# Moving PE transposes in and out of a saturated matmul stream at both ends of a six-layer cross network, and issuing the last stores from three engines

## The chip, the cores and the metric

One core of a Trainium2 chip. The metric is the device time of one execution in microseconds (us), read as the median over several executions.

In the profile, PE is TensorE's matmuls, PEld its weight loads, DVE VectorE, ACT ScalarE, POOL GpSimd, SP SyncE. The letter q behind an engine means its sequencer. The "span" is the time from the first to the last instruction; the measured time of a profiled run is about 1.8 us longer than its span.

## The reference

```python
B, D, L = 16384, 1024, 6            # all tensors bfloat16
def reference(x0, ws, bs):          # x0 (B, D), ws (L, D, D), bs (L, D)
    x = x0
    for l in range(ws.shape[0]):
        x = x0 * (x @ ws[l] + bs[l]) + x
    return x
```

## The kernel before

The batch is cut into 16 blocks of 1024 rows. Everything is computed transposed: features lie on the partitions and batch rows in the free dimension, so that the output of one layer is directly the moving operand of the next. A block has two halves of 512 rows (`bc`) and eight output groups (`nt`) per half. A group is eight accumulating matmuls of 128x512 into one PSUM bank, followed by two DVE operations.

```python
def layer(blk, l, x0T, src, dst, o_nat):
    for bc in range(BC):                       # 2 halves of 512 rows
        cs = slice(bc * MM_N, (bc + 1) * MM_N)
        for nt in range(NT):                   # 8 output groups
            ps = psum.tile([P, MM_N], FP32, name="ps", tag="ps")   # 8 buffers, shared
            for kc in range(KT):               # 8 matmuls
                nc.tensor.matmul(ps[:], lhsT=w_sb[l][:, kc, nt * P : (nt + 1) * P],
                                 rhs=src[:, kc, cs], start=(kc == 0), stop=(kc == KT - 1))
            # DVE: tmp = (ps + bias) * x0T ;  dst = tmp + src
            ...
            if last_layer and last_blk:        # progressive transposes back to rows
                for m in range(MS):            # 4 row tiles of this half
                    if nt % TPB == 0:
                        pts[m] = psum.tile([P, TPB, P], BF16, name="pt", tag="ps")
                    nc.tensor.transpose(pts[m][:, nt % TPB, :], dst[:, nt, col : col + P], ident[:])
                    if nt % TPB == TPB - 1 or nt == NT - 1:
                        ...                    # stage tile "on" at the first
                        evac_copy(on[:, j0 : j0 + nj, :], pts[m][:, :nj, :])   # ACT, DVE in turn
                        if nt == NT - 1:
                            nc.sync.dma_start(out=out[r : r + P, :], in_=...)  # 256 KB
```

The other 15 blocks are transposed in and out by DMA, off the critical path. Only the first block's input is transposed by TensorE, all of it ahead of the first layer:

```python
for s in range(MS): load_rows(s)               # row tiles 0..3, 256 KB each, on SP
load_w(0, 0, half)                             # first half of W0, 1 MB
load_w(0, half, D)                             # second half
for s in range(MS, BS): load_rows(s)           # row tiles 4..7
for l in range(1, L): load_w(l, 0, D)
...                                            # bias
for s in range(BS):
    pe_transpose_in(x0T_next, s, x0_rows[s])   # 8 transposes + one copy, per row tile
for blk in range(NBLK): ...                    # the layers
```

The scheduler of the compiler moves instructions within an engine. In the last layer it puts the four transposes of a group behind the sixth matmul of the next group, not directly behind their own.

## Time and profile before

| | before |
|---|---|
| median of 12 runs | 2689.27 us (2687.78 to 2689.86) |
| span of the profiled run | 2688.0 us |
| TensorE busy | 99% |
| first layer matmul | 17.74 us |
| full TensorE clock granted from | 20.09 us |
| last group's matmuls done to the end of the span | 7.5 us |

The time of the full clock is where the trace's clock record opens. It has no entry for the stretch before, and the page's PEclk row shows that stretch as full; that the clock was half there is read from the matmuls, which come every 0.43 us until then. (The prediction below says that the record "is 0.5"; it means this.)

From the page of the kernel before: the span, the busy shares, and the chain of work that ended last by engine and by line.

```profile
span 2688.0 us, 28374 instructions
...
PE 2654.2 (99%) x12177; PEld 1211.8 (45%) x12424; DVE 1811.0 (67%) x3081; ACT 9.2 (0%) x9; POOL 0.7 (0%) x6
...
PE 99%; issue 1%; DMA 0%; DVE 0%; ACTq 0%; ACT 0%
```

The matmul stream is the limit. In it one matmul follows another every 10.79/50 = 0.2158 us, and 12,288 of them make 2652 us. A change that keeps the matmuls can only act on the remaining 36 us at the two ends. The head is read from the chain of waits, kernel before, first 30 us (columns: start, duration, what):

```profile
3.52 1.06 PE pt L108 x9
4.59 9.72 DMA xn<-in_x_dram
14.31 0.05 issue
14.36 3.60 PE pt L108 x32
17.95 0.43 PE ps L133
```

TensorE waits for row tile 4 of x0 (`xn`) until 14.36, transposes rows 4 to 7 (L108, 32 transposes in 3.60 us on the slow clock), and only then starts layer 0 (L133). The landing events of the trace say that the first half of W0 had been there since 10.63 us.

The tail: the waits of TensorE in the kernel before, the whole span (columns: engine and line, what it waited for, us in total, times, longest; two lines of the start, 2.6 and 0.2 us, are left out).

```profile
PE pt L108 <- DMA xn<-in_x_dram: 7.6, 3, 6.2
PE pt L161 <- DVE xT L149: 4.4, 3, 1.8
```

The second line is three stalls of the last layer's transposes (L161): 1.30 us at 2645.3, 1.83 us at 2663.7 and 1.30 us at 2680.5. One regular step of the last layer, from the timeline of the kernel before (start, duration, engine, line, operation, in brackets the idle time before it and what ended it):

```profile
2668.95 0.23 PEld L161 LDWEIGHTS <-xT 128*128 128x128 bf16 x4 [0.50 <-DVE xT L149]
2668.96 0.40 PE L161 MATMUL pt<-ident,xT 128*128 128x128 bf16 x4
...
2669.19 1.89 PE L133 MATMUL ps<-xT,w 128*128 128x512 bf16 x8
...
2670.61 0.42 DVE L149 TENSOR_TENSOR xT<-tmp,xT 128x512 bf16<-128x512 bf16 x1
2671.09 0.23 PEld L161 LDWEIGHTS <-xT 128*128 128x128 bf16 x4 [0.50 <-DVE xT L149]
2671.09 0.40 PE L161 MATMUL pt<-ident,xT 128*128 128x128 bf16 x4
```

A step is 2671.09 - 2668.96 = 2.13 us for eight matmuls (8 x 0.2158 = 1.73 us) and four transposes. A matmul's bar is 0.38 us long though the next one can start 0.216 us later (its end is modelled).

### The profile page before, as it was taken

What the parts mean: (1) busy time and instruction counts of PE and PEld (TensorE: products, weight loads), DVE (VectorE), ACT (ScalarE), POOL (GpSimd) and SP (SyncE); (2) the same over time, 40 slices, a digit from 0 to 9 for tenths busy, and PEclk for the clock granted to TensorE, in tenths of its full rate; (3) what the DMA queues carried; (4) which work ended last, traced back from release to release, by engine and by line L of the source; (5) the groups of instructions that cost most, each with busy time, mean ns of one, the idle gap of its engine ahead of it and who ended that gap; (6) DMA issues with size and microseconds to landing.
All of it is one profiled execution on the core that took longest, in us unless ns stands there. A gap on an engine that the chain in (4) does not pass through costs nothing.

```text
span 2688.0 us, 28374 instructions
## 1 busy us (share of the span) xinstructions
PE 2654.2 (99%) x12177; PEld 1211.8 (45%) x12424; DVE 1811.0 (67%) x3081; ACT 9.2 (0%) x9; POOL 0.7 (0%) x6
## 2 busy tenths in 40 slices
PE   8999999999999999999999999999999999999998
PEld 4444444444444444444444444444444444444443
DVE  5666666666666666666666666666666666666665
ACT  0000000000000000000000000000000000000000
POOL 0000000000000000000000000000000000000000
PEclk9999999999999999999999999999999999999999
DMA  8030030300303012030120302203021030210200
GB/s 250 1 81 14 11 84 1 94 1 16 79 0 94 1 33 62 1 95 1 41 54 1 94 1 46 49 1 95 0 58 38 1 94 0 63 32 7 57 1 32
DMA packets 279962, 113.03 MB, mean 42 GB/s; under 512 B 255254, under 2 KB 257302, under 8 KB 279836
## 3 DMA queue, kind: packets, MB, share of 16 engines
q10 hardware_dynamic: 146412, 62.96, 9.5%
q1 hardware_dynamic: 133424, 48.24, 7.2%
q8 instruction: 97, 1.59, 0.3%
q14 instruction: 29, 0.24, 0.0%
HBM read 14.69 MB, written 33.55 MB: 18 GB/s over the span
## 4 chain that ended last, share of the span: by engine, by line
PE 99%; issue 1%; DMA 0%; DVE 0%; ACTq 0%; ACT 0%
PE ps L133 98%; DMA xn<-in_x_dram 0%; PE pt L161 0%; PE pt L108 0%; DVE tmp L141 0%; ACTq L229 0%; DVE on L100 0%; DVE xT L149 0%; ACT on L98 0%
## 5 line engine op out<-in xcount | busy, mean ns | idle before, releaser
L133 PE MATMUL ps<-xT,w 128*128 128x512 bf16 x10033 | 2204.0, 379 | 10.8
L133 PEld LDWEIGHTS <-w 128*128 128x128 bf16 x12288 | 1202.0, 98 | 1446.9 <-issue 1.5
L141 DVE SCALAR_TENSOR_TENSOR tmp<-ps,bias_sb,x0T 128x512 bf16<-128x512 f32 x1536 | 1153.2, 751 | 803.1 <-PE ps L133 771.6
L149 DVE TENSOR_TENSOR xT<-tmp,xT 128x512 bf16<-128x512 bf16 x1280 | 543.6, 425 | 44.0
L133 PE MATMUL ps<-x0T,w 128*128 128x512 bf16 x2008 | 443.5, 380 | 2.3 <-issue 0.2
L149 DVE TENSOR_TENSOR xT<-tmp,x0T 128x512 bf16<-128x512 bf16 x256 | 108.7, 425 | 8.8
L108 PE MATMUL pt<-ident,xn 128*128 128x128 bf16 x64 | 7.4, 313 | 7.6 <-DMA xn<-in_x_dram 7.6
L98 ACT COPY on<-pt 128x1024 bf16<-128x1024 bf16 x4 | 3.9, 1015 | 2661.9 <-PE pt L161 2661.9
L100 DVE COPY x0T<-pt 128x1024 bf16<-128x1024 bf16 x4 | 2.8, 692 | 12.7 <-PE pt L108 12.7
L161 PE MATMUL pt<-ident,xT 128*128 128x128 bf16 x64 | 6.4, 222 | 4.6 <-DVE xT L149 4.4
L108 PEld LDWEIGHTS <-xn 128*128 128x128 bf16 x64 | 6.6, 148 | 8.2 <-DMA xn<-in_x_dram 8.2
L161 PEld LDWEIGHTS <-xT 128*128 128x128 bf16 x64 | 3.6, 97 | 12.4 <-DVE xT L149 12.4
L98 ACT COPY x0T<-pt 128x1024 bf16<-128x1024 bf16 x4 | 4.1, 1013 | 11.5 <-PE pt L108 11.5
L100 DVE COPY on<-pt 128x1024 bf16<-128x1024 bf16 x4 | 2.7, 685 | 0.8 <-PE pt L161 0.8
L84 PE MATMUL bias_ps<-ident,bs_nat 6*128 6x6 bf16 x8 | 0.4, 165 | 2.6 <-DMA bs_nat<-in_bs_dram 2.6
L92 DVE COPY bias_sb<-bias_ps 128x48 f32<-128x48 f32 x1 | 0.2, 208 | 3.0 <-PE bias_ps L84 3.0
L84 PEld LDWEIGHTS <-bs_nat 6*128 6x128 bf16 x8 | 0.3, 101 | 2.6 <-DMA bs_nat<-in_bs_dram 2.6
L98 ACT ACT_TABLE_LOAD x1 | 1.3, 1283 | 1.4 <-PEq L218 1.4
masks.py:199 POOL TENSOR_SCALAR_AFFINE_SELECT ident<-ident 128x128 bf16<-128x128 bf16 x1 | 0.3, 295 | 0.1
masks.py:197 POOL MEMSET ident<- 128x128 bf16 x1 | 0.2, 205 | 0.3 <-POOLq L218 0.3
L218 POOL MEMSET const-bfloat16-1.0<- 128x1 bf16 x1 | 0.1, 103 | 0.0
L218 POOL MEMSET const-uint8-127<- 128x1 uint8 x1 | 0.1, 103 | 0.0
(2 smaller groups left out, 0.2 us busy)
## 6 DMA issues: line engine op xcount, KB each, us to landing
out_dram<-o_nat ACTq DMA_DIRECT2D x30, 1024.0 KB, 4.5
w<-in_ws_dram SPq DMA_DIRECT2D x5, 2048.0 KB, 19.9
o_nat<-xT ACTq DMA_TRANSPOSE x240, 2.4
xn<-in_x_dram SPq DMA_DIRECT2D x8, 256.0 KB, 4.6
w<-in_ws_dram SPq DMA_DIRECT2D x2, 1024.0 KB, 9.0
out_dram<-on SPq DMA_DIRECT2D x8, 256.0 KB, 2.3
x0T<-in_x_dram SPq DMA_TRANSPOSE x30, 7.9
bs_nat<-in_bs_dram ACTq DMA_DIRECT2D x1, 12.0 KB
```

What stands on the lines that cost most here:

```text
L84: nc.tensor.matmul(bias_ps[:, j, :], lhsT=bs_nat[:, j * P : (j + 1) * P], rhs=ident[0:L, 0:L], start=True, stop=True,)
L92: nc.vector.tensor_copy(out=bias_sb[:], in_=bias_ps[:])
L98: nc.scalar.copy(out=out_ap, in_=in_ap)
L100: nc.vector.tensor_copy(out=out_ap, in_=in_ap)
L108: nc.tensor.transpose(pt[:, jj, :], xn[:, (j0 + jj) * P : (j0 + jj + 1) * P], ident[:])
L133: nc.tensor.matmul(ps[:], lhsT=w_sb[l][:, kc, nt * P : (nt + 1) * P], rhs=src[:, kc, cs], start=(kc == 0), stop=(kc == KT - 1),)
L141: nc.vector.scalar_tensor_tensor(out=tmp[:], in0=ps[:], scalar=bias_sb[:, nt, l : l + 1], in1=x0T[:, nt, cs], op0=ALU.add, op1=ALU.mult,)
L149: nc.vector.tensor_tensor(out=dst[:, nt, cs], in0=tmp[:], in1=src[:, nt, cs], op=ALU.add)
L161: nc.tensor.transpose(pts[m][:, nt % TPB, :], dst[:, nt, col : col + P], ident[:])
L218: nc = _bacc.Bacc("TRN2", target_bir_lowering=False, num_devices=1)
```

## The change

Its intent is to start layer 0 as soon as rows 0 to 3 and W0 are there, and to transpose rows 4 to 7 inside layer 0's first half; to transpose the last layer's first half in one block; and to spread the last stores over three issuing engines. Eight stage buffers instead of four were meant to let rows 4 to 7 be requested early.

```diff
-    stage = ctx.enter_context(tc.tile_pool(name="stage", bufs=4))
+    stage = ctx.enter_context(tc.tile_pool(name="stage", bufs=8))
 ...
+    out_q = [nc.sync, nc.scalar, nc.gpsimd]        # store_rows(r, on): in turn
 ...   in layer():
+            progressive = last_layer and last_blk and bc == BC - 1
 ...
+                if after_group is not None and (bc, nt) in after_group:
+                    after_group[(bc, nt)]()
-                if last_layer and last_blk:
+                if progressive:                    # second half only
                     for m in range(MS):
 ...
-                            evac_copy(on[:, j0 : j0 + nj, :], pts[m][:, :nj, :])
+                            if nt == NT - 1 and m % 2 == 1:
+                                nc.vector.tensor_copy(out=on[...], in_=pts[m][...])
+                            else:
+                                nc.scalar.copy(out=on[...], in_=pts[m][...])
+                                store_rows(b0 + col, on)          # at nt == NT - 1
+            if last_layer and last_blk and not progressive:       # first half: one block
+                for m in range(MS):
+                    ...   # 8 transposes, one ACT copy, store_rows
 ...
-    for s in range(BS):
+    for s in range(MS):
         pe_transpose_in(x0T_next, s, x0_rows[s])
+    # rows 4..7: hooks of layer 0, first half, behind groups nt = 2, 3, 5, 6
+    after0 = {(0, nt): transposes of one row tile ...}
```

In the compiled order of the changed kernel, the block of 32 transposes has the 21 that do not need the half's last DVE result in front, and the other 11 behind them.

More of the change, by code (lines that the diff above doesn't have):

```diff
@@ L121, in load_block_T_dma, with store_rows, layer @@
         return x0T
-    def layer(blk, l, x0T, src, dst, o_nat):
+    out_q = [nc.sync, nc.scalar, nc.gpsimd]
+    out_rr = [0]
+    def store_rows(r, on):
+        q = out_q[out_rr[0] % len(out_q)]
+        out_rr[0] += 1
+        q.dma_start(out=out[r : r + P, :], in_=on[:].rearrange("p j c -> p (j c)"))
+    def layer(blk, l, x0T, src, dst, o_nat, after_group=None):
         last_layer = l == L - 1
@@ L167, in layer @@
                             if j0 == 0:
-                                on = stage.tile([P, KT, P], BF16, name="on", tag="xn")
-                                pts[(m, "on")] = on
+                                pts[(m, "on")] = stage.tile([P, KT, P], BF16, name="on", tag="xn")
                             on = pts[(m, "on")]
-                            evac_copy(on[:, j0 : j0 + nj, :], pts[m][:, :nj, :])
+                            if nt == NT - 1 and m % 2 == 1:
+                                nc.vector.tensor_copy(out=on[:, j0 : j0 + nj, :], in_=pts[m][:, :nj, :])
+                            else:
+                                nc.scalar.copy(out=on[:, j0 : j0 + nj, :], in_=pts[m][:, :nj, :])
                             if nt == NT - 1:
-                                r = b0 + col
-                                nc.sync.dma_start(
-                                    out=out[r : r + P, :],
-                                    in_=on[:].rearrange("p j c -> p (j c)"),
-                                )
+                                store_rows(b0 + col, on)
             if last_layer and not last_blk:
@@ L186, in layer @@
                 )
+            if last_layer and last_blk and not progressive:
+                for m in range(MS):
+                    col = bc * MM_N + m * P
+                    on = stage.tile([P, KT, P], BF16, name="on", tag="xn")
+                    for j0 in range(0, KT, TPB):
+                        nj = min(TPB, KT - j0)
+                        pt = psum.tile([P, TPB, P], BF16, name="pt", tag="ps")
+                        for jj in range(nj):
+                            nc.tensor.transpose(
+                                pt[:, jj, :], dst[:, j0 + jj, col : col + P], ident[:]
+                            )
+                        nc.scalar.copy(out=on[:, j0 : j0 + nj, :], in_=pt[:, :nj, :])
+                    store_rows(b0 + col, on)
     x0T_next = x0pool.tile([P, KT, Bb], BF16, name="x0T", tag="x0T")
-    for s in range(BS):
+    for s in range(MS):
         pe_transpose_in(x0T_next, s, x0_rows[s])
+    hooks0 = {}
+    rest = list(range(MS, BS))
+    if rest:
+        slots = [(0, nt) for nt in range(min(2, NT - 1), NT)]
+        for i, s in enumerate(rest):
+            key = slots[min(i * len(slots) // len(rest), len(slots) - 1)]
+            hooks0.setdefault(key, []).append(s)
+    x0T_blk0 = x0T_next
+    after0 = {
+        k: (lambda ss=ss: [pe_transpose_in(x0T_blk0, s, x0_rows[s]) for s in ss])
+        for k, ss in hooks0.items()
+    }
     for blk in range(NBLK):
@@ L199 @@
                 o_nat = opool.tile([P, BS, KT, P], BF16, name="o_nat", tag="o_nat")
-            layer(blk, l, x0T, src, dst, o_nat)
+            layer(blk, l, x0T, src, dst, o_nat, after_group=after0 if (blk == 0 and l == 0) else None)
             src = dst
```

## The prediction

> **What bounds the kernel.** The matmul stream. The page shows TensorE 99% busy over the 2688.0 us span, and the chain of waits puts 98.2% on the layer matmuls. In the timeline a matmul of 128x512 follows the one before it every 10.79/50 = 0.2158 us; 12,288 of them make 2652 us, which the change does not touch. Only about 36 us lie outside: a head of 17.74 us before the first layer matmul, its slow first matmuls, the transposes of the last layer, three stalls there, and 7.5 us from the last matmul to the end. DVE (67%), ACT and DMA (mean 42 GB/s) are not limits.
>
> **Head.** The chain shows: TensorE waits until 14.36 us for row tile 4 of x0, transposes rows 4 to 7 (3.60 us), then starts layer 0. Its own inputs were there earlier: row tiles 0 to 3 are transposed and copied by 8.9 us and, by the landing events, the first half of W0 landed at 10.63 us (second half 13.63, rows 4 to 7 at 14.31 to 16.34). After the change layer 0 can start at about 10.7 us: 7.0 us earlier. I expect no change in the landings: same queue, same order, and the loads are limited by 350 to 390 GB/s. Given back:
> - The 32 transposes move into the stream: in the last layer four cost 0.40 us between matmuls, so 32 cost 3.2 us.
> - The slow clock. The Trainium skill, "TensorE: Matmul & The Clock Gate", Part 1, says that the array starts at half rate and is released only by a busy window of about 3.4 us. The trace agrees in kind: the clock record is 0.5 until 20.1 us, 5.7 us after TensorE restarted at 14.36, and matmuls come every 0.43 us until then. Before, 2.4 us of matmuls ran slow (1.2 us lost). After, TensorE restarts at 10.7 with matmuls themselves, and 3.4 to 6.8 us run slow: 1.7 to 3.4 us lost, some 1.4 us more.
> Net: 7.0 - 3.2 - 1.4 = 2.4 us. The evacuations of these transposes fit beside layer 0's (1.2 of 1.73 us of DVE per group).
>
> **Tail.** The timeline shows TensorE idle 1.30 us at 2645.3 (transposes right behind their DVE), 1.83 us plus a broken group at 2663.2 (PSUM buffers wait for copies), and 1.30 us before the last transposes. After: the first half runs without transposes, then 32 in a block (the compiled order puts 21 that don't need the last tile first, so no stall); one 1.3 us stall remains behind the first group of the second half, and the final 1.3. So 12.1 + 3.2 + 1.7 + 1.3 + 2.8 + 12.1 = 33.2 us from the end of the first group to the last matmul, against 35.15: 1.9 us gained.
> Last stores: now 4 on SP, issues 0.45 us apart, last landing 2686.92, 4.9 us after the first copy. After, ACT does two copies of 1.01 us and only then issues two stores: about 4.9 us again. No gain; GpSimd's store may cost a little. I take -0.1 us.
>
> **Sum.** 2.4 + 1.9 - 0.1 = 4.2 us, 0.16%: predicted 2685.2 us, range 2683.0 to 2687.8. Faster by over 2%: 1%; within 2%: 98%; slower: 1%.
>
> **To look for.** First layer matmul at 10.5 to 11 us; full clock granted between 14 and 18 us; eight-transpose packets of about 0.8 us inside layer 0 without waits on DMA; no idle TensorE at the start of the last layer; about 1.3 us behind the first group of its second half; the last landing about 6.4 us after the last matmul.
>
> **What would make it wrong.** W0 landing later because rows 4 to 7 and W1 are requested earlier; a late clock release; a stall of the transposes on their copies; a GpSimd store that ends last.

## The result, and the profile after

| | before | after |
|---|---|---|
| median | 2689.27 us (12 runs) | 2682.69 us (10 runs, 2681.59 to 2684.33) |
| span of the profiled run | 2688.0 us | 2681.1 us |
| first layer matmul | 17.74 us | 11.16 us |
| full clock from | 20.09 us | 14.69 us |
| last group's matmuls done to the end | 7.5 us | 7.8 us |

The ratio is 0.9976, 95% interval 0.9967 to 0.9985. A ratio here is the mean time of one kernel's fast runs over that of the other's of the same rounds, so it is not quite the ratio of the medians. The change is clear of the noise and far below 2%. The predicted 2685.2 us and its range (from 2683.0) were too slow: 6.6 us were gained where 4.2 had been forecast.

The head after, from the chain of waits of the changed kernel, first 60 us:

```profile
2.81 8.30 DMA w<-in_ws_dram
11.12 0.05 issue
11.16 3.84 PE ps L142 x9
15.00 0.05 issue
15.06 3.19 PE ps L142 x14
18.24 0.45 PE pt L108 x8
18.69 1.73 PE ps L142 x8
20.41 0.45 PE pt L108 x8
```

The start now waits for W0 instead of x0. The first matmuls run slow (nine in 3.84 us). Eight transposes inside the stream then take 0.45 us of the chain. The waits of TensorE after the change, whole span (the first line, the bias matmuls' wait of 2.7 us, is left out):

```profile
PE pt L172 <- DVE xT L158: 2.6, 2, 1.3
PE ps L142 <- DMA w<-in_ws_dram: 2.5, 1, 2.5
PE pt L108 <- DMA xn<-in_x_dram: 1.7, 3, 0.7
```

Two stalls of the last layer are left of three. The block of 32 transposes, from the timeline of the changed kernel:

```profile
2653.03 2.26 PE L204 MATMUL pt<-ident,xT 128*128 128x128 bf16 x32
2653.23 0.75 DVE L150 SCALAR_TENSOR_TENSOR tmp<-ps,bias_sb,x0T 128x512 bf16<-128x512 f32 x1 [0.52 <-PE ps L142]
2654.01 0.42 DVE L158 TENSOR_TENSOR xT<-tmp,xT 128x512 bf16<-128x512 bf16 x1
2654.49 0.62 PEld L204 LDWEIGHTS <-xT 128*128 128x128 bf16 x11 [0.31 <-DVE xT L158]
...
2655.34 1.67 PE L142 MATMUL ps<-xT,w 128*128 128x512 bf16 x7
...
2657.05 0.75 DVE L150 SCALAR_TENSOR_TENSOR tmp<-ps,bias_sb,x0T 128x512 bf16<-128x512 f32 x1 [2.61 <-PE ps L142]
```

One matmul of that group has no record (7 of 8), so the block's cost is better read between the DVE operations that each group releases: 2657.05 - 2653.23 = 3.82 us, less 1.73 us of matmuls, is 2.09 us for 32 transposes, a wait of 0.3 us included.

The whole difference of the two spans, taken apart. As marks I use the first layer matmul, the start of the DVE operation behind the last group of layer 0, and the same for the first and the last group of the last layer:

| stretch | before | after | difference |
|---|---|---|---|
| start to first layer matmul | 17.74 | 11.16 | -6.58 |
| layer 0 without its slow-clock loss | 27.82 | 29.58 | +1.76 |
| slow-clock loss: half of (full clock minus first layer matmul) | 1.18 | 1.77 | +0.59 |
| layer 1 to the last layer's first group | 2598.63 | 2598.63 | 0.00 |
| last layer's first group to its last | 35.12 | 32.14 | -2.98 |
| last group to the end | 7.52 | 7.83 | +0.31 |
| sum | 2688.0 | 2681.1 | -6.9 |

"Half" because a matmul comes every 0.43 us on the slow clock and every 0.216 us on the full one.

### The profile page after: what moved, and what is told of

Its sections match the earlier page's. It is cut to its first block, busy times and chain, and to the rows that moved or that the text cites. A ratio compares the mean times of both kernels' runs of the same rounds, so it can differ in the third digit from the quotient of the medians.

```text
span 2681.1 us, 28362 instructions
## 1 busy us (share of the span) xinstructions
PE 2652.3 (99%) x12177; PEld 1211.0 (45%) x12424; DVE 1809.9 (68%) x3079; ACT 11.0 (0%) x11; POOL 1.9 (0%) x8
## 3 DMA queue, kind: packets, MB, share of 16 engines
HBM read 14.69 MB, written 33.55 MB: 18 GB/s over the span
## 4 chain that ended last, share of the span: by engine, by line
PE 99%; issue 1%; DMA 0%; DVE 0%; ACT 0%; SPq 0%
PE ps L142 99%; DMA w<-in_ws_dram 0%; PE pt L172 0%; DVE tmp L150 0%; ACT on L184 0%; SPq L59 0%; PE pt L108 0%; DVE xT L158 0%; PE pt L204 0%
```

## The experiments

Ten kernels were run, each for five rounds beside the kernel before on the same chip. All gave correct results. Theory A is the table above: a transpose inside the stream costs 0.056 us. Theory B is the prediction's: it costs 0.10 us anywhere, and what is left over came from a lucky clock in one profile.

| run | edit against the changed kernel | median, us | before, us | ratio (95%) |
|---|---|---|---|---|
| head_only | tail of before | 2685.49 | 2688.66 | 0.9984 (0.9971 to 0.9998) |
| tail_only | head of before | 2686.34 | 2688.66 | 0.9989 (0.9977 to 1.0002) |
| double_t | rows 4 to 7 transposed twice | 2684.42 | 2688.66 | 0.9982 (0.9969 to 0.9994) |
| sp_stores | all last stores on SP | 2682.10 | 2688.66 | 0.9973 (0.9960 to 0.9985) |
| stage4 | four stage buffers | 2683.38 | 2689.08 | 0.9976 (0.9964 to 0.9989) |
| lag_t | last transposes one group later | 2679.61 | 2689.08 | 0.9964 (0.9952 to 0.9977) |
| w0_quarters | first half of W0 in two loads | 2682.01 | 2689.08 | 0.9971 (0.9958 to 0.9983) |
| warm | ten unread matmuls ahead of layer 0 | 2680.85 | 2689.08 | 0.9969 (0.9955 to 0.9982) |
| combined | lag_t, sp_stores, w0_quarters, nine unread matmuls | 2676.18 | 2689.03 | 0.9952 (0.9939 to 0.9966) |
| after_again | none (control) | 2682.74 | 2689.03 | 0.9977 (0.9964 to 0.9989) |

### Head alone and tail alone

```diff
 head_only: kernel before, with   bufs=8, after_group hooks, transposes of rows 4..7 in layer 0
 tail_only: changed kernel, with  bufs=4 and
-    for s in range(MS): pe_transpose_in(...)     # and hooks
+    for s in range(BS): pe_transpose_in(...)     # no hooks
```

> The head of the change (rows 4 to 7 transposed inside layer 0, eight stage buffers) on the tail and stores of before. Theory A, from the two traces: a transpose inside a warm matmul stream costs 0.056 us (eight took 0.445 us), so the head alone gains about 4.2 us (first layer matmul 6.6 us earlier, 1.8 us of transposes given back, 0.6 us more slow clock), give or take 0.9 us for the moment at which the clock is released: 2685.1 us. Theory B, the prediction's: a transpose costs 0.10 us anywhere, and the rest was a lucky clock in one profile: 2.4 us gained, 2686.9 us. In the trace: A sees 0.44 us between the last matmul start of a group and the next group's, beyond 0.216, per eight transposes; B sees 0.8.

> The tail of the change (block of 32 transposes for the first half, progressive for the second, stores on three queues) on the head of before, four stage buffers. Theory A: 2.98 us gained up to the last matmul (two stalls gone and the block costs 2.1 us with its wait, not 3.2), 0.3 us lost in the stores: about 2.7 us faster than before, 2686.6 us. Theory B: 1.8 us faster, 2687.5 us. First layer matmul at 17.7 us as before for both.

Head alone gained 3.2 us in the medians, tail alone 2.3 us. Both lie between the two theories, so the times alone do not decide. The traces do. In head_only the tail is that of before, to 0.01 us (16.24 + 2.20 + 16.69 = 35.13 us from the first to the last group of the last layer, against 35.12). In tail_only it is that of the changed kernel (12.09 + 3.82 + 16.23 = 32.14). So the two parts don't interact. The profiled run of head_only gained 3.4 us in its span, and what made it less than 4.2 is in its trace too: the clock was released 4.79 us behind the first layer matmul, not 3.53, and W0 landed at 11.35 us. Its layer 0 without the slow-clock loss is 29.58 us, the same as in the changed kernel.

### Each transpose twice

```diff
-            for jj in range(nj):
+            for jj in [jj for _ in range(2 if s >= MS else 1) for jj in range(nj)]:
                 nc.tensor.transpose(pt[:, jj, :], xn[...], ident[:])
```

> The changed kernel with each of the 32 transposes of rows 4 to 7 done twice in place (same result). Theory A: 32 more transposes in the stream cost 32 x 0.056 = 1.8 us: 2684.5 us, and a packet of sixteen takes 0.89 us of the stream. Theory B: 3.2 us, 2685.9 us, and 1.6 us per packet.

2684.42 us against the changed kernel's 2682.69: 1.7 us for 32 more transposes, as theory A said. From the chain of waits of double_t, first 40 us:

```profile
15.06 3.19 PE ps L142 x14
18.25 0.89 PE pt L108 x16
19.14 1.73 PE ps L142 x8
20.87 0.89 PE pt L108 x16
```

Sixteen take 0.89 us, eight took 0.45. Layer 0 without its slow-clock loss reads 27.82, 29.58 and 31.38 us with 0, 32 and 64 transposes in it: 1.76 and 1.80 us for each 32, or 0.055 to 0.056 us apiece. Theory B is refuted.

### Why four transposes had looked like 0.40 us

```diff
-   transposes of group nt emitted behind group nt
+   transposes of group nt - 1 emitted behind group nt; at the last group both
```

> The changed kernel with each group of four transposes in the last half placed one matmul group later, so that it finds its DVE result ready. Theory A: the 0.40 us that four transposes took in the last layer is 4 x 0.056 = 0.22 us of transposes and 0.18 us of waiting for DVE and for the exposed weight load; then six or seven groups shrink from 2.13 to about 1.95 us (about 1.1 us), and the 1.3 us stall behind the first group of that half goes: 2.4 us faster than the changed kernel, 2680.3 us. Theory B: a transpose costs 0.10 us: only the stall goes, 1.3 us faster, 2681.4 us, and groups stay 2.13 us apart.

From the timeline of lag_t, the same step as shown of before:

```profile
2661.05 0.43 PEld L174 LDWEIGHTS <-xT 128*128 128x128 bf16 x4
2661.26 0.39 PE L174 MATMUL pt<-ident,xT 128*128 128x128 bf16 x4
...
2661.49 1.89 PE L142 MATMUL ps<-xT,w 128*128 128x512 bf16 x8
...
2663.00 0.43 PEld L174 LDWEIGHTS <-xT 128*128 128x128 bf16 x4
2663.22 0.39 PE L174 MATMUL pt<-ident,xT 128*128 128x128 bf16 x4
```

The idle note on the weight load is gone, and a step is 1.96 us instead of 2.13. The transposes are the same, so 0.18 us of the earlier 0.40 was waiting for DVE: the weight load of the first transpose is the DVE result itself, and it was ready only about 0.2 us after TensorE had wanted it. (The expectation also named the exposed weight load; lag_t removes both together and does not part them.) From the first to the last group of the second half the trace has 13.43 us instead of 16.23, that is 2.8 us less. Of it, 1.3 us is the stall behind the first group that vanished, 6 x 0.18 = 1.1 us the six remaining steps, and 0.4 us the seventh packet, which now stands behind the last matmul, where TensorE waits anyway (1.08 us of idle are left there, where it was 1.30). The median fell by 3.1 us.

### The stores

```diff
-    out_q = [nc.sync, nc.scalar, nc.gpsimd]
+    out_q = [nc.sync]
```

> The changed kernel with all eight last stores issued by SP. If spreading them over three queues is worth something (the intent of the change), this is slower: the last landing later than 6.73 us after the last layer's final DVE operation began. Theory A: the last four landings of before were 0.68 us apart, which is 256 KB at 385 GB/s, so the transfers and not the issues set the end; all on SP lands at about 6.4 us after that point as before, about 0.3 us faster than the changed kernel: 2682.4 us, too small for the times but visible in the landings.

The stretch from the last group to the end is 7.46 us, against 7.83 in the changed kernel and 7.52 before; the last landing comes 6.38 us behind that group's first DVE operation, against 6.72 and 6.43. The time, 2682.10 us, differs from 2682.69 in the expected direction but within the noise. The other traces agree: the stretch is 7.83 to 7.89 us in the eight with three issuing engines and 7.41 to 7.52 in the four with SP alone. Spreading the stores therefore pays nothing and costs about 0.35 us. Behind the mark, which is the start of that DVE operation, the last four stores land at 4.33, 5.02, 5.71 and 6.38 us with SP alone and at 4.65, 5.69, 6.20 and 6.72 in the changed kernel: 2.05 and 2.07 us from first to last, so the transfers form one train, whoever issues them. The Trainium skill, "DMA: Bandwidth & Descriptors", section "Issuing engines are not separate DMA queues", states that DMAs of all issuing engines run on the same 16 DMA engines and that several issuers save only issue time; this trace agrees. What moved the train, as I read the issue times, is its first store. With SP alone that store is issued 2.31 us behind the mark; with three queues SP has no early one: ACT issues at 2.57 and GpSimd at 2.59. GpSimd's own issue is also longer, as the profile of the output tile in the changed kernel shows (columns: engine, operation, count, issue time min/median/max in ns):

```profile
L129 SPq DMA_DIRECT2D out_dram<-on x3: 332/350/363, 2655.8 to 2676.8; - x3
...
L129 POOL DMA_DIRECT2D out_dram<-on x2: 542/610/679, 2657.9 to 2675.9; - x2
```

### Does the early request of rows 4 to 7 delay W0?

```diff
-    stage = ctx.enter_context(tc.tile_pool(name="stage", bufs=8))
+    stage = ctx.enter_context(tc.tile_pool(name="stage", bufs=4))
```

> The changed kernel with four stage buffers, so that rows 4 to 7 are requested only as rows 0 to 3 are used up, as before the change. In the four traces with eight buffers the first half of W0 landed at 11.02 to 11.40 us, in the two with four at 10.51 and 10.63. Theory A: the early requests delay it, so here it lands at 10.5 to 10.7 and layer 0 starts about 0.5 us sooner, 0.4 us off the total: 2682.2 us. Rival: the landing varies from run to run whatever the buffers are, and it lands anywhere in 10.5 to 11.4.

My theory fell. The first half of W0 landed at 11.44 us with four buffers. Over all traces in which it is one load it landed between 10.31 and 11.69 us, with four buffers at 10.51, 10.63 and 11.44, and with eight at 10.31, 10.38, 11.02, 11.12, 11.35, 11.40 and 11.69. It varies from run to run; no effect of the buffers is visible. The experiment had little to change, though: SP requested rows 4 to 7 at 4.59, 7.20, 8.18 and 8.65 us in the kernel before, at 4.29, 7.96, 8.63 and 9.22 in the changed one and at 4.59, 8.70, 9.16 and 9.66 in stage4. With eight buffers SP spent 3.63 us on issuing row 4, and the others came no earlier than before. What a really early request would do to W0 is not tested. The time (2683.38) is that of the changed kernel.

### W0 in smaller pieces, and the clock

```diff
-    load_w(0, 0, half)
+    load_w(0, 0, half // 2)
+    load_w(0, half // 2, half)
```

> The changed kernel with the first half of W0 loaded as two quarters. If the start is bound by that load, the first quarter lands about 1.4 us earlier (512 KB at 350 GB/s or more), at about 9.8 us, and the first layer matmul moves with it; the total gains 1.4 us if the clock release moves along, and only about 0.7 us if the release stays where it was: 2681.3 to 2682.0 us.

The first quarter landed at 9.36 us and the first layer matmul came at 9.41. The median gained only 0.7 us, which is not clear of the noise: the five runs spread over 3.1 us (2679.64 to 2682.71), and three of them lie among those of the changed kernel. The profiled run was the fastest of them, and its clock record shows why: full clock from 7.84 us, before the first layer matmul, where the changed kernel had 14.69. In the chain of waits of w0_quarters, first 20 us, the first nine matmuls then take 2.12 us instead of 3.84:

```profile
9.36 0.05 issue
9.41 2.12 PE ps L143 x9
```

The start 1.75 us earlier and the slow-clock loss of 1.77 us saved make up the profiled run's gain (3.2 us of span), less 0.2 us in which the transposes of row 4 now wait for its landing. The clock of the other four runs is not on record; that it was released later in them is my reading, not shown. An earlier start is worth less when the clock is released no earlier, since matmuls run at half speed until then (0.43 against 0.216 us each). The control shows it: in after_again W0 landed 0.74 us sooner than in the first profile of this kernel, the release came 0.41 us later, and the spans differ by 0.16 us.

```diff
+    warm(3, zeros)                       # ahead of the bias
     for s in range(MS):
         pe_transpose_in(x0T_next, s, x0_rows[s])
+        warm((0, 0, 1, 6)[s], x0_rows[s])   # matmuls 128x512 into a PSUM tile nobody reads
```

> The changed kernel with ten matmuls that nobody reads (three before the bias, one behind the transposes of row 2, six behind those of row 3), to keep TensorE busy until W0 lands. If activity releases the clock, the release comes before or soon after the first layer matmul (under 1 us behind it, against 2.96 to 4.79 us in the traces of the changed head) and up to 1.8 us of slow matmuls is saved, about 1.3 us in the mean: 2681.4 us. If the release is tied to something else, it stays at 14 to 16 us and the total is the same or up to 0.4 us longer.

The clock was released at 6.46 us, 3.9 us before the first layer matmul. The median fell by 1.8 us, and all five runs (2680.39 to 2681.35) are faster than the fastest of the changed kernel's fifteen, control included (2681.59). One early release could be chance, since w0_quarters had one without unread matmuls; five faster runs speak against it. A narrower spread is not shown: the five lie within 1.0 us of each other and the ten of the changed kernel within 2.7, but the five of the control within 0.6. From the chain of waits of warm, first 20 us: all 24 matmuls ahead of the first transposes come at full rate.

```profile
10.31 0.04 issue
10.36 5.35 PE ps L152 x24
15.71 0.45 PE pt L118 x8
```

A first build of this kernel was not run: the scheduler had moved all ten unread matmuls to the front, because they shared one PSUM tile. One tile per place, and the row tile as operand, kept them where they were meant to be.

### Together, and a control

> The changed kernel with what the runs so far showed to pay: transposes of the last half one group later (2.8 us in the trace), all last stores from SP (0.37 us), quarters of W0 (first layer matmul about 1.7 us sooner) and nine unread matmuls to warm the clock (up to 1.8 us, and a narrower spread). If they add up, 2682.7 - 6.6 = 2676.1 us; if quarters and warm matmuls hide one another's gain, about 2677.5 us. Full clock before the first layer matmul, at 9.4 to 10 us.

> The changed kernel itself once more, as a control on the same chip as the combined one and as one more sample of the clock's release: 2682.7 us; release 2.9 to 4.8 us behind the first layer matmul, which itself comes at 10.4 to 11.8 us by the landing of W0.

The combined kernel took 2676.18 us, 12.9 us under before and 6.6 us under the changed kernel of the same rounds; its ratio 0.9952 has an interval (to 0.9966) that just touches that of the changed kernel (0.9964 to 0.9989), while the runs themselves do not overlap (2675.51 to 2678.37 against 2682.58 to 2683.14). Its profiled run was the slowest of five (2678.37 us): row 3 landed late (8.02 us), TensorE stood idle 0.8 us before it, and the release came at 12.60 us, 2.0 us behind the first layer matmul. My expectation of a full clock before layer 0 thus failed in that run. The unread matmuls even cost something there: the first quarter of W0 had landed at 9.82 us, but the four behind row 3, on the slow clock, held TensorE until the first layer matmul at 10.60. Nine unread matmuls do not always warm the clock in time; how often they do was not measured. The control gave 2682.74 us, the changed kernel's time.

## Why the prediction was right or wrong

- **What bounds the kernel**: right. The 2598.63 us between layer 0 and the last layer are the same to 0.01 us in all twelve traces.
- **Earlier start, 7.0 us**: 6.58 us. W0 landed 0.5 us later in this run (11.12 against 10.63 us), which is within the run-to-run scatter that stage4 and the control show.
- **"four cost 0.40 us between matmuls, so 32 cost 3.2 us"**: wrong, and this is the step that failed. The 32 transposes in layer 0 cost 1.76 us. The 0.40 us per four was 0.22 us of transposes and 0.18 us of waiting for DVE; lag_t took the wait away and double_t measured the transpose alone. The line that shows it, the 0.50 us of PEld idle ended by DVE, was there in the profile of before. I read the PE row, whose overlapping bars hide it. The same wrong figure sits in the tail's sum: the block was put at 3.2 us and took 2.09. Together the two terms are 1.4 + 1.1 = 2.5 us.
- **Slow clock, "some 1.4 us more"**: 0.59 us more. The mechanism was right and the size off: I had estimated 3.4 to 6.8 us of slow matmuls (one to two of the windows that the prediction cites), and the changed head, in seven traces that keep its loads as they are apart from the buffers, showed 2.96 to 4.79 us. The 0.59 us is partly luck: by the mean of the seven, 3.91 us, it would be 0.8 us, and before's own 2.35 us is one draw too (tail_only, with the same head, had 1.00).
- **Tail stalls**: right in kind. The first stall went, the second, behind the first group of the second half, shrank from 1.83 us to 1.31, and 1.30 us before the last transposes remained.
- **Last stores, -0.1 us**: the right sign; 0.3 us.

The sum of the errors, in us: 1.4 (transposes of layer 0) + 1.1 (block) + 0.8 (clock) - 0.4 (start) - 0.2 (stores) = 2.7, which is the gap between the forecast 4.2 and the 6.9 of the spans. With the transposes priced right the forecast would have been 4.2 + 2.5 = 6.7 us; that this is so close is luck in part, since the other three errors nearly cancel.

## What to carry to other kernels

Before pricing an instruction by the period of a loop that contains it, look whether that period contains a wait: on TensorE the weight-load row shows it, and the matmul row can hide it under overlapping bars. In a saturated matmul stream PE transposes are cheap (0.056 us each here), so they belong inside the stream, one group later than looks natural, so that their DVE input is ready. At a start bound by loads, an earlier first matmul pays in full only if the clock is warm by then. Keeping TensorE busy while it waits helped in warm, but in the profiled run of combined it did not warm the clock in time.

## What the Trainium skill lacked or had wrong

- "TensorE: Matmul & The Clock Gate", Part 4, says that transposes do not engage the full clock. In w0_quarters the clock was released at 7.84 us, 1.6 us before the first layer matmul, after nothing but transposes (3.49 to 7.85 us) and eight tiny bias matmuls; in tail_only it came 1.00 us behind the first layer matmul, with 32 transposes in front. TensorE had done no other work before the release in w0_quarters, so transposes count as activity here, if these are what the page means: the profile calls them MATMUL and does not tell the mode. They do not always suffice: in the seven traces of the changed head the same 32 were in front, and the release came after layer 0's start.
- The same page, section "Back-to-back issue gap", gives about 0.081 us (N=128) and 0.131 us (N=512) per matmul as the sustained rate of streams with weight loads, and calls N / 2.4 + 2.5 ns the isolated case. Here streams with a weight load for every matmul ran at 0.2158 us (N=512) and 0.056 us per transpose (N=128), which is the "isolated" formula. Part 1 of that page has the same 55.6 and 215.7 ns for back-to-back matmuls, so only this section is off.
- The same page, Part 1, puts the release behind a busy window of about 3.4 us. The clock records agree with that length: in all twelve traces the full clock, once granted, was held for a whole number (779 to 782) of stretches of 3.4133 us. For the changed head it came 2.96, 3.53, 3.57, 3.87, 3.98, 4.67 and 4.79 us behind the first layer matmul; the page's remark that the moment depends on the run is confirmed. How busy a window must be is not stated: with gaps of up to 0.8 us among transposes and unread matmuls, the combined kernel's profiled run was not released until 12.60 us.
- The same page, Part 4, writes a transpose as in.T @ identity, which makes the data the weight load. It does not draw the consequence for reading a trace: a short wait for a late producer shows as idle time of the weight loads and not of the matmuls (0.50 us noted on PEld, none on PE), and it cost 0.18 us per group of four here.
- No page that I read gives the scatter of load landings at the start of a program: the same 1 MB landed between 10.31 and 11.69 us in ten traces, with no effect of the number of stage buffers visible.
